# Raw projection weights for two chunks, paired transposes, sums parked through VectorE, and a new order in a fused attention and token-mixing block

## The chip, the core and the metric

The kernel runs on one core of a Trainium2 chip. The core has four compute engines that this kernel uses: TensorE (PE in the profile; its weight loads are shown apart as PEld), VectorE (DVE), ScalarE (ACT) and GpSimd (POOL). SyncE (SP) issues nearly all DMAs. Each engine works through its own instructions in program order and waits at semaphores for the others. The metric is the device time of one launch in microseconds, as the median of several runs.

## The reference

One residual block with two branches on x of 2048 tokens and 512 features, all in bf16. Six rows (sa, ca, ga, sb, cb, gb) come from a condition vector:

```python
mod = (_silu(c) @ w_mod).reshape(c.shape[0], 6, 1, -1)
h = _layernorm(x) * (1 + ca) + sa
x = x + ga * A(h)      # attention
h = _layernorm(x) * (1 + cb) + sb
x = x + gb * B(h)      # token mixing
```

Branch A projects h to q, k and v (32 heads of 16), and lets every position attend to 8 earlier positions at distance 0, 2, ... 14 of its own head; then comes the projection wo. Branch B takes a further layer norm of h, multiplies over the tokens: u = w1ᵀ h (2048 tokens to 1792 rows), adds b1, applies gelu, and comes back with y = w2ᵀ u + b2 (1792 to 2048).

## The kernel before

The 2048 tokens are 16 tiles of 128. Attention runs in five chunks of 2, 4, 4, 4 and 2 tiles (`SIZES`). Of each chunk, in names that stand in the order (chunk number first):

- ln1s, rstd1, nb1, n1: the first layer norm. ln1s takes a tile's statistics (on VectorE `bn_stats` and, at once behind it, `bn_aggr`; for tiles 10 to 13 on ScalarE with two passes that accumulate), n1 writes the normalized tile.
- tr, hT: for chunks 0 and 1 the transpose by TensorE and its copies out of PSUM. For chunks 2 to 4 it is xt, a DMA transpose of each tile on SP's queue.
- qkv{chunk}_{t}{j}, ev: projections (t = 0 for q, 1 for k, 2 for v) and their eviction. The scale 1 + ca (`a1col`) is folded into the weights: wsc multiplies each quarter of the loaded weights `wraw` by it and writes `w_r`. The shift sa goes into biases qvb of q and v, made by TensorE from the raw weights.
- vd: a DMA that spreads v; qk: products of q and shifted k on VectorE (up to 4096 elements a partition); red: their sums over the head on TensorE; max, sub, exp, esum, rcp, smB: the softmax; a2: DMAs that spread the probabilities; pv, pvacc, oev: products with v, sums, eviction. Chunk c needs the last 16 positions of the chunk before, copied by halo_k and halo_v.
- wo, x1: the output projection. The residual is added as one more product with the identity, except for tiles 14 and 15, where VectorE adds it. ln2q, ln2m, ln2s, n2, aff and ln3s, n3 (h3): second and third layer norms with the affine map between them.

Branch B runs in sweeps. mlp1_{sweep}_{row tile}_{first token tile} sums u over tokens. Row tiles 0 to 6 are summed over tokens 0 to 5, then 6 to 10, then 11 to 15; row tiles 7 to 13 over 0 to 9 and 10 to 15. A sum that isn't complete is parked as bf16 in `gT` (park, a copy). In the second of three sweeps the parked sum comes back into PSUM as a product with the identity (inj1_0 to inj1_6) before the sweep's own products; in a last sweep VectorE adds it (padd) and gelu follows. mlp2_{token tile} is the second product, fin adds b2, gb and the residual, st_out stores.

Rows of gates and shifts (modcol, mcols, mrowt, mrows) are made as columns with 64 products of one column, copied, transposed by TensorE, copied, stored and loaded back as broadcast rows. Warm-up bursts (warm0 to warm3, nine small products each) and fill keep TensorE running.

Nothing of the order is found at run time: the string `ORDER` (lines 182 to 238) lists every step by name, and steps are issued to their engines in that order. A letter behind a name picks the engine (:a ScalarE, :d VectorE), :q splits a product in four of 32 columns that run side by side. Slots of PSUM (`psS`, six), of `big` and of `vD` are given out in the same pass. The engine of each normalized tile stands in the strings `NE`, one letter a tile. The profile puts every operation on line 133, the wrapper that records it, so it is read by tiles.

Of the kernel before, what the change touches and what calls it, by code (L numbers as in the profile page):

```python
# [13 lines left out]
P = 128  # L14
# [27 lines left out]
class _Graph:  # L42
# [42 lines left out]
    def schedule(self):  # L85
# [4 lines left out]
        for pos, token in enumerate(ORDER.split()):  # L90
            name, *rest = token.split(":")
            if name == "fill":
                k, n = map(int, rest)
# [5 lines left out]
            o.quad = rest == ["q"]  # L99
            assert all(d in done for d in o.deps), name  # L100
            for eng, dur, fn in o.alts:
                if rest and eng[0] == rest[0]:
                    o.eng, o.dur, o.fn = eng, dur, fn
# [79 lines left out]
consts ld_x_1_2 act_table ld_x0 ld_x_1_4 ld_c ld_x_2_8 ld_x1 ident ld_x_2_6 ld_wmod1 ln1s3 halo0 ld_wqkv1 cps  # L183
ln1s2 warm2 ld_wqkv0 silu_exp ld_wmod0 ln1s0 ln1s4 ln1s1 ln1s5 rstd1_0 ld_x_4_14 nb1_0 ln1s9 rstd1_1 n1_0 n1_1
silu_dve nb1_1 ld_wqkv2 ln1s8 fill:2:70 tr0_0 n1_2 n1_4 modcols1 ln1s7 hT0_3:a n1_5 n1_3 ld_x_3_10 hT0_2:d a1col
hT0_0:a fill:4:16 tr1_2 wsc1_2:d ld_b1 hT0_1:a wsc1_3:d wsc1_0:a tr1_0 wsc1_1:d ln1s6 hT1_2:a ld_wmod2 qkv0_10
ld_x_3_12 wsc0_0:d rstd1_2 wsc0_1:d qkv0_12 wsc0_2:d hT1_1:a nb1_2 n1_8 n1_9 wsc0_3:d modcols0 hT1_0:d ld_wmod3
hT1_3:a qkv0_00 sab ev0_12:d n1_6 ld_wmod4 qvb0 ln1s14 ld_wo1 qkv0_02 qvb_cp0 ln1s15 ev0_00:a wsc2_2 qvb1
wsc2_0:d qkv1_00 wsc2_3 ev0_10:a ev0_02:d ln1s10 wsc2_1:d qkv1_10 qvb_cp1 qk0_0 ev1_10:a qkv0_22 qk0_1 n1_7
qkv0_20 ln1s13 qk0_2 qkv1_02 xt6 red0_0 ev1_00:a qk0_3 red0_1 red0_2 ev0_22:a ld_wmod5 qkv1_22 qk1_0 ev0_20:a  # L190
qkv1_12 ev1_02:a vd0_1 red0_3 ev1_12:a mask qkv1_11 vd0_0 ln1s11 max0 xt8 qk1_2 qkv1_01 ev1_11:a sub0 qkv1_03
ev1_01:a xt9 exp0 qkv1_13 qk1_1 ev1_03:a xt7 esum0 ev1_13:a qkv1_20 rcp0 vd0_2 ln1s12 qkv1_21 smB0 qk1_3 a2_0_3
modcol2 rstd1_4 qkv1_23 a2_0_0 ev1_22:a a2_0_2 halo_v1:a red1_0 ev1_20:a a2_0_1 red1_1 ln1v10 ln1v12 ln1v11
ln1v13 nb1_4 red1_2 rstd1_3 n1_15 ld_wo3 red1_3 nb1_3 ld_wo2 mcols0 n1_11 n1_10 qkv2_00 max1 ev1_21:a n1_14 xt10
qkv2_02 ev2_00:a pv0_0 qkv2_10 n1_12 ld_wo0 pv0_1 qkv2_11 vd0_3 ev2_10:a ev2_02:a qkv2_12 qk2_0 n1_13 qkv2_01
xt12 ev2_12:a pvacc0_0 ev2_01:a sub1 qk2_2 xt13 qkv2_03 exp1 qkv2_13 xt11 ev2_11:a ev2_03:a qkv2_22 qk2_1
ev2_13:a esum1 ev1_23:a qkv2_21 rcp1 vd1_2 red2_0 smB1 ev2_21:a ld_b2 red2_1 qk2_3 halo_v2:a a2_1_1 red2_2
pvacc0_1 a2_1_3 qkv3_00 a2_1_2 qkv3_10 a2_1_0 pv0_2 mrowt0 vd1_1 qkv2_20 ev3_10:a pv0_3 ev3_00:a red2_3 mrows0:a
qkv2_23 ev2_20:a st_row0 max2 halo_k3:p ev2_22:a vd1_3 qkv3_11 qk3_0 xt14 qkv3_22 ev3_11:a pvacc0_2 ld_row0
pvacc0_3 sub2:q oev0_2:a vd1_0 pv1_2 qkv3_02:q exp2 qkv3_12 ev3_02:a ev2_23:a qkv3_01 pv1_3 oev0_0:a vd2_2 esum2  # L200
modcol3 xt15 rcp2 ev3_12:a woq_s qkv3_20 ev3_01:a pvacc1_3 smB2 ev3_20:a red3_0 qk3_1 ev3_22:a a2_2_0 pvacc1_2
wo1 a2_2_1 vd2_3 qkv3_13:q x1_1 a2_2_2 pv1_1 vd2_1 wo0 ev3_13:a a2_2_3 qkv4_02 ld_w1_0_512 oev1_2:a mcols1 pv1_0
ld_w1_0_0 oev1_3:a mrowt1 qkv3_03 mrows1:a x1_0 st_row1 qkv4_00 ev3_03:a vd2_0 ln2q1 qk3_2 pvacc1_0 ev4_02:a
red3_1 pvacc1_1 oev1_0:a qkv3_23:q oev1_1:a qk3_3 ev4_00:a wo3:q ln2q0 wo5:q pv2_2 qkv4_22:q x1_5 ev3_23:a wo2:q
ld_row1 ln2q5 ld_w1_0_896 ln2m0 halo_v3:a wo4:q x1_3 pv2_1 x1_2 red3_2 x1_4 red3_3 ln2q3 qkv3_21:q pv2_3 rstd2_0
qkv4_20 ln2q2 ev3_21:a ev4_22:a vd3_3 pvacc2_1 nb2_0 max3 pvacc2_2 n2_0 warm0 ln2q4 vd3_0 n2_1 ln2m2 sub3 pv2_0
# [35 lines left out]
def kernel(  # L242
# [373 lines left out]
    def build_chunk(ch):  # L616
# [113 lines left out]
        if ch == 2:  # L730
            halo(3, "k")
# [307 lines left out]
```

## Time and profile before

| | us |
|---|---|
| median of 3 runs (lowest to highest) | 207.07 (206.38 to 207.98) |
| span of the profiled execution | 204.6 |
| busy: PE, DVE, ACT, POOL | 194.7, 163.3, 120.6, 13.0 |
| mean DMA share of 16 engines, bytes moved | 61.4%, 35.67 MB on the main queue |

The span runs from the first to the last instruction. A busy PE is not PE at its peak: matmuls are pipelined, and the time of one (0.38 us for 512 columns) is longer than the distance to the next. Further views are the stretches (busy time of each engine between two times), the chain of waits (the work that ended last, followed back), the timeline and the groups by shape.

### The profile page before, as it was taken

The numbers are of one execution on the slowest core, as the hardware profiler recorded it, in microseconds if no ns is written. First come the engines' busy times: TensorE is split into PE (matmuls) and PEld (weight loads), VectorE is DVE, ScalarE is ACT, GpSimd is POOL, SyncE is SP. The second block draws the span as 40 slices with busy tenths as digits, with TensorE's granted clock in tenths as the row PEclk, the third lists the DMA queues.
The fourth block names the chain that finished last, engine by engine and source line by source line (L and its number), as shares of the span: only waits on it lengthen the run. The fifth ranks groups of instructions, "written<-read, shape, count | busy, mean of one in ns | idle before, by whom it ended". The sixth has DMA issues, their size and how long they took to land.

```text
span 204.6 us, 4223 instructions
## 1 busy us (share of the span) xinstructions
PE 194.7 (95%) x1655; PEld 103.5 (51%) x1655; DVE 163.3 (80%) x260; ACT 120.6 (59%) x283; POOL 13.0 (6%) x36
## 2 busy tenths in 40 slices
PE   3999999999999997989899999999999999999994
PEld 3988554454455553554344445444444444444453
DVE  2899999999999999999999999975473204369365
ACT  2398998994666899989898876683762000000000
POOL 4122001100000001240000000100000000000000
PEclk9999999999999999999999999999999999999999
DMA  5999494646958976194975179946990930121121
GB/s 141 330 380 348 117 239 107 161 98 201 247 186 267 308 234 251 25 272 110 289 200 115 26 157 263 288 131 200 340 304 3 232 88 16 39 77 51 51 82 51
DMA packets 55111, 35.93 MB, mean 176 GB/s; under 512 B 24628, under 2 KB 52404, under 8 KB 55092
## 3 DMA queue, kind: packets, MB, share of 16 engines
q1 hardware_dynamic: 55084, 35.67, 61.4%
q8 instruction: 13, 0.21, 0.4%
q14 instruction: 6, 0.05, 0.1%
q10 hardware_dynamic: 8, 0.00, 0.0%
HBM read 22.55 MB, written 2.10 MB: 121 GB/s over the span
## 4 chain that ended last, share of the span: by engine, by line
PE 65%; DVE 20%; issue 5%; DMA 5%; SPq 3%; ACT 2%; DVEq 0%
PE psS L133 62%; DVE big L133 9%; DVE h L133 3%; PE psL L133 3%; SPq L133 3%; DVE st L133 3%; DMA wst<-in_B_w_dram 2%; DMA xx<-in_A_x_dram 2%; ACT h L133 1%; DVE mv L133 1%; DVE m L133 1%; DVE lsb L133 1%; DVE ls L133 0%; DVE nb L133 0%; DVE woq L133 0%
## 5 line engine op out<-in xcount | busy, mean ns | idle before, releaser
L133 PE MATMUL psS<-h,wst 128*128 128x512 bf16 (+1 forms) x254 | 50.7, 379 | 1.2 <-POOL h L133 0.7
L133 PE MATMUL psS<-hT,w_qkv 128*128 128x512 bf16 (+3 forms) x312 | 46.2, 339 | 0.3 <-ACT w_qkv L133 0.3
L133 PEld LDWEIGHTS <-wst 128*128 128x128 bf16 (+1 forms) x356 | 28.7, 98 | 32.2 <-issue 3.2
L133 PEld LDWEIGHTS <-w_qkv 128*128 128x128 bf16 (+1 forms) x354 | 29.5, 111 | 21.3 <-issue 3.2
L133 DVE TENSOR_TENSOR big<-a2sb,vD 128x4096 bf16<-128x4096 bf16 (+1 forms) x20 | 36.9, 1876 | 0.0
L133 DVE TENSOR_TENSOR big<-q_sb,k_f 128x4096 bf16<-128x4096 bf16 (+1 forms) x20 | 36.3, 1857 | 0.0
L133 DVE SCALAR_TENSOR_TENSOR h<-psS,bcol,rows_bc 128x512 f32<-128x512 f32 (+2 forms) x18 | 12.4, 690 | 24.4 <-PE psS L133 24.2
L133 PE MATMUL psS<-gT,big 128*128 128x512 bf16 x112 | 24.8, 379 | 0.0
L133 PEld LDWEIGHTS <-big 128*128 128x128 bf16 x144 | 12.0, 97 | 13.2
L133 PEld LDWEIGHTS <-ident 128*128 128x128 bf16 (+1 forms) x203 | 13.9, 111 | 5.9 <-issue 2.8
L133 PE MATMUL psS<-woq,o_sb 128*32 128x512 bf16 (+1 forms) x172 | 16.6, 380 | 0.0
L133 ACT ACTIVATE h<-xx,nb,rs 128x512 bf16<-128x512 bf16 x19 | 15.0, 807 | 0.8 <-DVE nb L133 0.7
L133 DVE TENSOR_TENSOR psS<-psS,gT 128x512 f32<-128x512 f32 x14 | 9.3, 696 | 7.0 <-PE psS L133 7.0
L133 ACT ACTIVATE junk<-xx 128x512 bf16<-128x512 bf16 x22 | 13.8, 626 | 0.2
L133 POOL TENSOR_SCALAR h<-xx,rs,nb 128x512 bf16<-128x512 bf16 x9 | 7.3, 813 | 101.3 <-DVE nb L133 84.0
L133 ACT ACTIVATE lv<-mv,epscol 128x1 f32<-128x1 f32 (+2 forms) x25 | 7.3, 291 | 9.3 <-DVE mv L133 8.4
L133 DVE BATCH_NORM_STATS2 st<-xx 128x6 f32<-128x512 bf16 x14 | 9.5, 678 | 4.0 <-DMA xx<-in_A_x_dram 4.0
L133 ACT ACTIVATE gT<-psS,bcol 128x512 bf16<-128x512 f32 x14 | 8.7, 688 | 6.4 <-DVE psS L133 6.4
L133 PEld LDWEIGHTS <-group 128*32 128x32 bf16 x288 | 6.8, 96 | 10.2 <-issue 4.8
L133 DVE TENSOR_TENSOR h<-h,rows_bc 128x512 bf16<-128x512 bf16 (+2 forms) x20 | 11.5, 581 | 0.5
L133 DVE TENSOR_TENSOR h<-h,xx 128x512 bf16<-128x512 f32 (+2 forms) x18 | 11.4, 633 | 0.6
L133 ACT ACTIVATE gT<-psS 128x512 bf16<-128x512 f32 x19 | 10.8, 587 | 1.6 <-PE psS L133 1.5
(94 smaller groups left out, 220.4 us busy)
## 6 DMA issues: line engine op xcount, KB each, us to landing
vD<-v_sb SPq DMA_DIRECT2D x12, 524.5 KB, 3.8
big<-in_B_w_dram SPq DMA_DIRECT2D x4, 896.0 KB, 8.2
vD<-v_sb SPq DMA_DIRECT2D x8, 268.5 KB, 3.0
wst<-in_B_w_dram SPq DMA_DIRECT2D x3, 640.0 KB, 5.3
out_dram<-h SPq DMA_DIRECT2D x15, 128.0 KB, 1.8
xx<-in_A_x_dram SPq DMA_DIRECT2D x7, 256.0 KB, 6.1
wst<-in_B_w_dram SPq DMA_DIRECT2D x2, 800.0 KB, 4.8
gT<-in_w_mod_dram SPq DMA_DIRECT2D x3, 512.0 KB, 6.1
```

The costliest lines, as they stand in the source:

```text
L133: r = fn(*a, **k)
```

## The change

- Chunks 0 and 1 are projected with the raw weights; the copies of their transposed tiles multiply by `a1col`. Only chunks 2 to 4 use `w_r`, and the twelve wsc move to GpSimd (7) and ScalarE (5); before, nine were on VectorE.
- One DMA transpose takes two tiles (five instead of ten), and its output lies tile by tile.
- The aggregate of the statistics is a step of its own in the order (ln1v, ln2v, ln3v). Statistics of the first and third norm can be on ScalarE: 3 of 16 and 8 of 16 are (before 4 and none).
- The engine of each normalized tile stands in the order: of n1, n2, h3 now 8, 8, 6 on ScalarE (before 9, 10, 8), 3, 6, 3 on VectorE (2, 2, 6) and 5, 2, 7 on GpSimd (5, 4, 2).
- An inj may be skipped (n); its park is then an addition on VectorE (+). All seven are. The residual product of a wo may be skipped in the same way, and x1 then adds it; this is used for tile 13.
- The rows of gates are made in rows at once: the condition column, broadcast to 32 columns, is the weight, and w_mod moves.
- halo_k3 comes after all q-k products of chunk 2, and runs on ScalarE; two v halos go from ScalarE to GpSimd. Five a2 DMAs are issued by ScalarE.
- The warm-up bursts are gone; fillers are 74 small products instead of 86, with a slot found by the pass. 42 products are split in four instead of 19.
- fin writes all three keys of its staging buffer where a tile has one piece. The whole order is new.

```diff
@@ schedule
-                k, n = map(int, rest)
+                n = int(rest[0])
+                k = min((freed["ps"][i], i) for i in range(self.pools["ps"]) if held["ps"][i] is None)[1]
...
+            flags = rest[0] if rest and o.eng == "pe" else ""
+            o.quad, o.skip = "q" in flags, "n" in flags
...
+            if o.eng == "pe":
+                o.eng, o.dur, o.fn = o.alts[o.skip]
...
+                if rest == ["+"]:
+                    o.eng, o.dur, o.fn = o.alts[-1]
@@ ln_stats
+        o = G.add_any([("dve", 0.68, fd)] + ([("act", 1.26, fa)] if l != 1 else []),
+                      reads=reads + (["act_table"] if l == 0 else []), writes=[("stt", l, st)], name=name)
...
+            if o.eng == "dve":
+                nc.vector.bn_aggr(mv[:, st, :], st6[:, st, :])
+            else:
+                nc.vector.scalar_tensor_tensor(mv[:, st, 1:2], mv[:, st, 0:1], mv[:, st, 0:1], st6[:, st, 0:1],
+                                               op0=ALU.mult, op1=ALU.subtract, reverse1=True)
@@ wraw: the value weights from h2_r[0] to h2_r[1]
-            wst[0][:, 0:KT * D].rearrange("p (k n) -> p k n", k=KT), h2_r[0][:, 0:KT, :])
+            wst[0][:, 0:KT * D].rearrange("p (k n) -> p k n", k=KT), h2_r[1][:, 0:KT, :])
@@ halo
-                  writes=[("kh", 3)] + [("k", -1, j) for j in range(4)] if nm == "k" else [("vh", ch), ("vh", ch - 2)],
+                  writes=[("kh", 3), ("kq", 2)] + [("k", -1, j) for j in range(4)] if nm == "k" else [("vh", ch), ("vh", ch - 2)],
@@ build_mod_rows
+                    for kt in range(KT):
+                        for dt_ in range(KT):
+                            nc.tensor.matmul(ps(s_)[32 * dt_:32 * dt_ + 32, r * P:(r + 1) * P],
+                                             lhsT=sc[:, kt:kt + 1].to_broadcast([P, 32]),
+                                             rhs=w_[:, kt, dt_ * P:(dt_ + 1) * P], start=(kt == 0), stop=(kt == KT - 1),
+                                             tile_position=(0, 32 * dt_))
@@ build_chunk: paired transposes
+            for sl in range(0, nt, XG):
+                st = t0 + sl
+                dma_t = lambda sl=sl, st=st: nc.sync.dma_start_transpose(
+                    out=hX[:, sl:sl + XG, :, :].rearrange("p s k q -> p (s k) q"),
+                    in_=h3[:, st:st + XG, :].rearrange("p s d -> p (s d)"))
@@ build_chunk: scaled copies, raw weights
+                    G.add_any([("act", _t_act(C, 1), lambda hd=hd, hs=hs, a_=a_: nc.scalar.activation(
+                        hd, hs(), ACT.Identity, scale=a_)),
+                               ("dve", 0.12 + 0.00052 * C, lambda hd=hd, hs=hs, a_=a_: nc.vector.tensor_scalar_mul(
+                                   hd, hs(), a_))], reads=["a1col"], writes=[("hT", bh, kt)], name=f"hT{ch}_{kt}",
...
-                        lhsT = _ap(w_r[t][:, kt, j:j + 1], [[4, P]])
+                        lhsT = _ap((wraw if ch in RAW else w_r)[t][:, kt, j:j + 1], [[4, P]])
@@ park
+                    fp = lambda s_=s_, ft=ft: nc.vector.tensor_tensor(gT[:, ft, :], ps(s_), gT[:, ft, :], op=ALU.add)
+                    G.add_any([("act", _t_act(D), fa), ("dve", _t_tt1(D), fd)] + ([("dve", 0.69, fp)] if inj else []),
+                              writes=[("gT", ft), "gT_use"], name=f"park{li}_{ft}", frees=s_).link = inj
@@ ORDER, its beginning and four later places
-consts ld_x_1_2 act_table ld_x0 ld_x_1_4 ld_c ld_x_2_8 ld_x1 ident ld_x_2_6 ld_wmod1 ln1s3 halo0 ld_wqkv1 cps
-ln1s2 warm2 ld_wqkv0 silu_exp ld_wmod0 ln1s0 ln1s4 ln1s1 ln1s5 rstd1_0 ld_x_4_14 nb1_0 ln1s9 rstd1_1 n1_0 n1_1
...
+ident ld_x_1_4 act_table ln1s4:d ld_x1 ld_x0 ld_x_1_2 ln1s1:d ln1v1 ln1v4 ld_wmod1 ld_c cps ln1s0:d ln1s5:a ln1v5
+fill:35 ln1v0 fill:14 ln1s2:d silu_exp consts rstd1_0 nb1_0 n1_0:a ln1s3:d n1_1:p ln1v2 ln1v3 silu_dve rstd1_1 nb1_1
+n1_5:d n1_4:d modcols1 tr0_0 a1col ld_x_2_8 n1_3:d n1_2:a tr1_0 hT0_1:a ln1s9:d ld_wqkv1 tr1_2 hT0_0:a hT1_0:d hT0_2:a
+ld_x_2_6 ln1s6:d hT0_3:a qkv0_12 hT1_3:a wsc1_1:p ld_wqkv0 hT1_2:a ld_x_3_12 ln1s7:d hT1_1:a ln1s8:d ln1v8 ev0_12:a
+ld_wmod0 wsc1_2:p wsc1_3:p ln1v7 ln1v6 qkv0_10 ld_x_3_10 ln1s13:d ln1v13 qkv1_13 wsc0_3:a ln1v9 ev0_10:a qkv0_02
...
+qkv1_12 mrows1 n1_8:p ev1_10:a qk1_0 qkv1_20 qkv1_23 xt8 vd0_2 a2_0_2:s qkv1_21:q qkv1_22:q ev1_12:a qk1_2 n1_11:a
+a2_0_1:a red1_0 qkv2_10:q qkv2_00:q red1_1 a2_0_3:s a2_0_0:s pv0_2 ln1s15:a ev1_22:a ev1_23:a st_row0 red1_2 red1_3
...
+mlp1_1_0_6 mlp1_1_0_10 ln2v14 rstd2_14 ld_w1_1_640 inj1_1:n mlp1_1_5_6 aff15 ln3s15:a nb2_14 park1_0:+ n2_14:p aff14
+inj1_4:qn mlp1_1_1_6 mlp1_1_6_6 inj1_3:qn rstd3_13 ld_w2_2 nb3_11 h3_11:p mlp1_1_3_6 mlp1_1_1_10 ln3v15 rstd3_15
...
+mlp2_11_0 st_out0_0 mlp2_8_0 mlp2_13_0 fin4_0 st_out4_0 fin7_0 st_out5_0 fin9_0 st_out9_0 mlp2_12_0 ld_w2_15 st_out7_0
...
+mlp2_15_2 mlp2_15_1 fin15_2 fill:7 fin15_1 st_out15_2 st_out15_1
```

292 lines of the change are left out of this document (128 added, 164 removed).

## The prediction

> **What bounds the kernel now.** I read the busy times by stretch first, then the chain of waits in order of time. Columns of the stretches: length, then busy time (and number of instructions) of TensorE, its weight loads, VectorE, ScalarE and GpSimd, the granted clock, the DMA share and GB/s.
>
> ```profile
> span 204.6 us, 4223 instructions
> ```
> ```profile
> 13.60:57.30 43.70, 43.69 (x404) 24.99 (x405) 43.41 (x52) 36.10 (x78) 3.41 (x5) 1.00 0.72 199
> 57.30:112.80 55.50, 51.97 (x656) 26.79 (x654) 54.64 (x68) 48.83 (x127) 4.22 (x5) 1.00 0.70 203
> 112.80:136.40 23.60, 23.57 (x137) 10.86 (x137) 22.18 (x63) 17.81 (x48) 0.77 (x1) 1.00 0.65 164
> 136.40:201.40 65.00, 65.00 (x330) 30.98 (x328) 33.09 (x50) 11.58 (x18) 0.00 (x0) 1.00 0.44 127
> ```
> ```profile
> 13.61 9.50 PE psS L133 x108
> ...
> 58.37 0.80 DVE woq L133
> ...
> 112.83 88.75 PE psS L133 x465
> ```
>
> TensorE is full in three of the four stretches, and the chain lies on it from 112.83 to the last product. But up to 112.8 VectorE is just as full (98.05 us of 99.2), and the chain lies on it from about 58 to 112. So two engines bind together up to the end of attention, TensorE alone after it. A gain needs less TensorE work or an earlier start, and VectorE must follow. The profiled span is 204.6 us, the median of the runs 207.07: 2.5 us lie outside the span and stay, so I subtract from 207.07.
>
> **Part 1, the start: raw weights and the new load order.**
>
> ```profile
> 12.17 0.15 DVE L133 TENSOR_SCALAR a1col<-psS 128x4 f32<-128x4 f32 x1
> 13.61 0.30 PE L133 MATMUL psS<-hT,w_qkv 128*128 128x256 bf16 x1 [0.26 <-ACT w_qkv L133]
> 19.48 1.21 DVE L133 TENSOR_TENSOR big<-q_sb,k_f 128x2048 bf16<-128x2048 bf16 x1
> ```
> ```profile
> L133 SPq DMA_DIRECT2D wst<-in_A_wqkv_dram x2: 505/542/578, 4.3 to 4.9; - x2
> ...
> DMA to landing us min/median/max: 7.0/7.4/7.8
> ```
> ```profile
> L133 SPq DMA_DIRECT2D xx<-in_A_x_dram x1: 1500/1500/1500, 7.1 to 7.1; - x1
> ...
> DMA to landing us min/median/max: 7.6/7.6/7.6
> ```
>
> Today the scale a1col (12.17) must multiply four weight slices before the first projection at 13.61. With raw weights for chunks 0 and 1 the copies of the transposed tiles carry the scale instead. Key and query weights landed at 4.3+7.0 = 11.3 and 4.9+7.8 = 12.7, when, by the sizes in the code, 2.30 and 2.82 MB had been asked for: 0.5 MB per 1.4 us. In the new order the key weights end at 2.05 MB, about 10.6, the w_mod half behind a1col at 1.28 MB instead of 1.79 (1.4 us earlier), and chunk 0's tiles at 0.51 MB instead of 1.02. I put a1col at 9.5 and four small copies behind it, first projection at 10.9: **-2.7 us for TensorE** (ends -3.0, the landing, and -1.0, if a1col moves little).
>
> VectorE's first q-k product (19.48) also needs the q bias, made from the other w_mod half. It ends at 3.58 MB, the same place in the queue as the x load that landed at 7.1+7.6 = 14.7. Column products, bias products, their copies and two evictions add some 3 us: 17.7, **-1.8 us for VectorE**. The nine weight slices that it loses fall in front of that point and are counted in it.
>
> **Part 2, TensorE's work.**
>
> ```profile
> 156.01 3.19 PE L133 MATMUL psS<-gT,big 128*128 128x512 bf16 x14
> ```
> ```profile
> 57.13 1.34 PE L133 MATMUL psS<-sc,gT 128*128 128x1 bf16 x48
> 58.33 1.04 PE L133 MATMUL psS<-hT,w_qkv 128*128 128x512 bf16 x4
> 59.30 0.61 PE L133 MATMUL psS<-big,group 128*32 128x512 bf16 x8
> ...
> 61.90 1.06 PE L133 MATMUL psS<-hT,w_qkv 128*32 128x512 bf16 x16
> ```
>
> A 512-column product costs (3.19-0.38)/13 = 0.216 us, 0.38 being the tail of the last. All seven inj tokens carry the flag that skips the identity product, and wo13 its residual one: 8 x 0.216 = -1.7. The 64 one-column products of modcol go (48 took 58.33-57.13 = 1.2 us, so 1.6); in come 64 quarter-width products of 128 columns, between 16 x 0.054 = 0.9 (four at a time) and 1.6 (none together). I take 1.2, as all quarter-width rows run four together: -0.4. A change between full and quarter width costs 0.1: the four at 58.33 need 0.97 instead of 0.86 until the quarter-width ones start. I count 38 changes instead of 34: +0.4. The 23 further tokens that split a product in quarters cost nothing (16 quarters at 61.90 take as long as 4 whole ones). Fillers are not counted; they stand where TensorE would wait. Sum **-1.7**; with the start -4.4.
>
> **Part 3, VectorE's work** between the first q-k product and the last normalized tile, which TensorE takes up with no slack today:
>
> ```profile
> 135.85 0.41 DVE L133 TENSOR_SCALAR h<-h,mv,rs 128x512 bf16<-128x512 bf16 x1 [0.30 <-ACT rs L133]
> ```
> ```profile
> 84.37 0.68 DVE L133 BATCH_NORM_STATS2 st<-h 128x6 f32<-128x512 bf16 x1
> 85.09 0.18 DVE L133 BATCH_NORM_AGGREGATE mv<-st 128x2 f32<-128x6 f32 x1
> 85.19 0.66 DVE L133 BATCH_NORM_STATS2 st<-h 128x6 f32<-128x512 bf16 x1
> ```
> ```profile
> L133 DVE SCALAR_TENSOR_TENSOR mv<-mv,st 128x1 f32<-128x1 f32 x4 | 0.6, 210 | 0.0
> ...
> L133 DVE TENSOR_TENSOR psS<-psS,gT 128x512 f32<-128x512 f32 x14 | 9.3, 696 | 7.0 <-PE psS L133 7.0
> ```
>
> A statistics pair takes 85.19-84.37 = 0.82; a next instruction that does not depend on the last starts 0.08 before its end. Eight pairs of this stretch go to ScalarE (-6.6), each leaving one small combine of 0.21-0.08 (+1.0). In the ten that stay the aggregate no longer stands right behind its statistics: 0.12 each, -1.2. Added: three parked sums before that tile, 3 x (0.70-0.08) = +1.9; x1_13, of a form that no row shows, bounded by that sum and by a statistics pair, +0.7; four more nb and the new row copies against the old column copies, +0.5. Sum -3.7.
>
> Against this stands GpSimd: 14 tile-sized operations in the stretch instead of 8 (h3 goes from 2 to 7), and 3 halo copies instead of 1.
>
> ```profile
> 36.01 0.77 POOL L133 TENSOR_SCALAR h<-xx,rs,nb 128x512 bf16<-128x512 bf16 x1
> ```
> ```profile
> 36.28 1.57 DVE L133 TENSOR_TENSOR big<-a2sb,vD 128x2048 bf16<-128x2048 bf16 x1
> ```
>
> The product at 36.28 began while GpSimd worked and took 1.57; one of its size took 1.21 at 19.48: +0.36. The bounds for the change are 0 (all beside statistics, as most are today) and 14 x 0.77 plus 3 copies, about 12. I take four collisions of 0.4, +1.6, nearer the low end because most of today's eight cost nothing. [...] VectorE in all: -1.8-3.7+1.6 = **-3.9**.
>
> **Part 4, what I cost at nothing.** ScalarE takes most of this work:
>
> ```profile
> 18.82 0.64 ACT L133 ACTIVATE junk<-xx 128x512 bf16<-128x512 bf16 x1
> 19.34 0.21 ACT L133 ACTIVATION_READ_ACCUMULATOR junk<-xx 128x1 f32 x1
> 19.58 0.63 ACT L133 ACTIVATE junk<-xx 128x512 bf16<-128x512 bf16 x1
> ```
> ```profile
> 0.83 0.56 ACTq L133 DMA_DIRECT2D c_t<-in_c_dram  x1
> ```
>
> One tile's statistics cost it 2 x (19.58-18.82) = 1.5 us; seven more in the stretch, five a2 issues of 0.56 (waiting for smB, with the evictions of the next projections queued behind), less its lost norms, parks and copies: some +10 on 102.7 of 122.8 busy. The cover is its 20 idle us, which become about 9 in a stretch that begins 2.7 and ends 4 us earlier; if that cover is gone, see the second rival.
>
> ```profile
> hT<-h SPq DMA_TRANSPOSE x10, 3.5
> ```
> ```profile
> L133 SPq DMA_TRANSPOSE hT<-h x10: 1211/1285/1714, 22.2 to 57.0; - x10
> ```
>
> A paired transpose holds SP's queue for 1.2 (as one) to 3.4 us (two of the slowest) and lands after 3.5 to 7. Between the issue of xt8 and the first chunk-2 projection TensorE has about three projections (12 x 0.216) and a reduction, some 3 us. I take one's cost; the other end is 3 us once, a2 and vd issues queued behind. The later key halo moves from GpSimd to ScalarE behind chunk 2's products, whose reductions already stand ahead of it. Parked sums after the last tile lie beside 65 us of full TensorE with 33 us of VectorE busy. The loads keep their queue; the late ld_w2_15 is issued some 9 us ahead of its use. fill:7 at the end stands beside the last output tile.
>
> The later of the two engines counts: -3.9 by VectorE, -4.4 by TensorE. I take -4.2: **202.9 us**.
>
> **Rivals.** *Full relief.* TensorE idles 3.5 us in 57.3 to 112.8 and does three warm-up bursts there; if VectorE gets ahead without collisions, another 4 us go: 198.9. For it: VectorE never waits today, so all that it loses counts. Against: its order was kept full by much ScalarE slack.
>
> *ScalarE becomes the bound.* If 12 of its 20 idle us stay, through dependent chains, the stretch lasts 113+12 = 125, 2.2 longer than now, and begins 2.7 earlier: no gain, 206.6. Against: those waits were mostly for a late VectorE.
>
> [...]
>
> *The clock.*
>
> ```profile
> 3.20:8.90 5.70, 5.70 (x55) 1.00 0.95 283
> 9.10:10.35 1.25, 1.25 (x26) 1.00 1.04 345
> ```
>
> Fillers start 0.104 us apart until 8.9 and about 0.05 after: TensorE ran at half pace until it had been busy for 5.9 us. The new start has 49 fillers, about 5.1 us at that pace, then a gap. If the change to full pace comes only after 5.9 us of unbroken projections, 3 us are lost: 205.9. [...]
>
> **Chances.** A measurement of this kernel tells about 1%, 2.1 us, from no change. Forecast (200.5 to 204.8) 0.45, full relief (198 to 200.5) 0.20, clock (204.5 to 206.5) 0.12, ScalarE (205.5 to 208) 0.12, port (208 to 213) 0.11. Faster, under 205.0: 0.45+0.20+0.05 = 0.70; slower, over 209.1: 0.10; the rest, 0.20, within. The range 198.3 to 207.8 leaves out the port and the best tenth.
>
> **What would show it.** First projection near 10.9 and first q-k product near 17.7; filler spacing before them; VectorE's products longer than 2.29 or 1.22 beside GpSimd; ScalarE's idle time up to the last normalized tile; the 65 us of TensorE after that tile unchanged. I am wrong if TensorE idles where it was full, between 13.6 and 57.3 or from 112.8 on.

## The result and the profile after

| | before | after |
|---|---|---|
| median, us (lowest to highest, 20 runs each) | 206.93 (206.05 to 207.98) | 205.28 (203.44 to 207.34) |
| profiled execution: time, span, us | 207.07, 204.6 | 207.27, 205.6 |

The ratio is 0.991, 95% interval 0.989 to 0.993: 1.65 us faster by the medians (about 1.9 by the ratio), where 4.2 was forecast. The profiled execution of the changed kernel is the second slowest of its 20; what is read from it below holds for that run, and the experiments' runs show what is usual. Six of the 20 runs, the profiled one among them, count as slow and are left out of the ratio, but not of the medians.

The page of the changed kernel, its span and the chain of waits by engine (before, PE had 65% of the chain, DVE 20% and ACT 2%):

```profile
span 205.6 us, 4632 instructions
...
PE 49%; ACT 19%; DVE 14%; DMA 7%; issue 6%; POOL 2%; SPq 1%; ACTq 0%; DVEq 0%; POOLq 0%
```

Its stretches, with the columns of the prediction's first table:

```profile
13.60:57.30 43.70, 41.74 (x569) 23.21 (x571) 39.38 (x45) 34.74 (x77) 8.35 (x11) 0.99 0.86 210
57.30:112.80 55.50, 52.17 (x721) 25.49 (x713) 54.63 (x65) 53.51 (x137) 2.50 (x4) 1.00 0.68 192
112.80:136.40 23.60, 23.27 (x135) 10.60 (x135) 21.80 (x63) 20.29 (x61) 4.59 (x6) 1.00 0.52 127
136.40:201.40 65.00, 65.00 (x326) 30.72 (x324) 34.91 (x53) 10.20 (x15) 0.00 (x0) 1.00 0.49 141
```

In the first stretch VectorE, full before (43.41 of 43.70 us), is busy for 39.38 us only, and TensorE has idle time too: the sign that the prediction named as its own refutation. In the second, three engines are now nearly full: ScalarE works 53.5 of 55.5 us.

To see where VectorE's relief went, take VectorE from its first q-k product to its last normalized tile. One row of that stretch for each kernel, before and then after; the fourth figure in each row is VectorE's busy time:

```profile
19.48:136.26 116.78, 113.22 (x1107) 57.14 (x1106) 114.47 (x162) 97.51 (x241) 7.04 (x9) 1.00 0.68 186
```
```profile
19.97:136.40 116.43, 111.07 (x1353) 54.56 (x1352) 111.67 (x157) 104.68 (x263) 11.70 (x14) 1.00 0.69 177
```

(The first figure is the length, the second TensorE, the third its weight loads.) The work fell by 114.47-111.67 = 2.8 us, more than the 2.1 forecast (-3.7+1.6). But the stretch is as long as before: VectorE idles 116.43-111.67 = 4.8 us where it idled 2.3, and it starts at 19.97, not at the 17.7 of the forecast. The largest wait and what lies behind it, from the waits of VectorE, SP's timeline and TensorE's timeline of the changed kernel:

```profile
DVE big L142 <- PE psL L142: 1.9, 1, 1.9
```
```profile
24.79 1.35 SPq L142 DMA_TRANSPOSE hT<-h  x1
26.19 0.75 SPq L142 DMA_DIRECT2D woq<-in_A_wo_dram  x1
26.98 0.58 SPq L142 DMA_DIRECT2D xx<-in_A_x_dram  x1
27.69 1.26 SPq L142 DMA_DIRECT2D vD<-v_sb  x2
29.05 1.52 SPq L142 DMA_TRANSPOSE hT<-h  x1
```
```profile
33.74 0.62 PE L142 MATMUL psL<-big,group 128*32 128x512 bf16 x8
35.22 1.06 PE L142 MATMUL psS<-hT,w_qkv 128*32 128x512 bf16 x16 [0.86 <-DMA hT<-h]
```

The second paired transpose (xt8) is issued at 29.05 behind two loads and two value copies and releases the projection at 35.22; TensorE stands 0.86 us, and as the reduction that frees VectorE's buffer is queued behind that projection, VectorE stands 1.9.

The late start shows in TensorE's granted clock (the figure after GpSimd's), in four stretches of the changed kernel:

```profile
7.70:9.10 1.40, 0.05 (x1) 0.10 (x1) 1.33 (x8) 1.23 (x3) 0.77 (x1) 1.00 0.95 322
9.10:11.30 2.20, 1.93 (x38) 1.62 (x38) 1.99 (x7) 1.88 (x5) 0.65 (x1) 1.00 1.07 375
11.40:14.70 3.30, 3.30 (x19) 2.41 (x17) 3.23 (x11) 3.30 (x7) 3.12 (x5) 0.50 1.11 382
14.80:17.00 2.20, 2.20 (x16) 1.61 (x15) 1.14 (x4) 1.60 (x4) 0.88 (x4) 1.00 1.08 355
```

The fillers end near 7.6 us, TensorE has next to nothing until 9.1, then column products and transposes run at full clock; and then, with TensorE full, the clock is at half for 3.4 us. The first two projections fall into it: at 11.53 and 13.24 they take 1.71 and 1.63 us for 0.86 us of work each. Of the 20 runs of the changed kernel, ten have a mean granted clock of 0.993 or less and a mean time of 206.3 us, and ten 0.998 or more and 204.8.

### The profile page after: what moved, and what is told of

Read it like the earlier page. It is cut to its first block, busy times and chain, and to the rows that moved or that the text cites. A ratio compares the mean times of both kernels' runs of the same rounds, so it can differ in the third digit from the quotient of the medians.

```text
span 205.6 us, 4632 instructions
## 1 busy us (share of the span) xinstructions
PE 192.8 (94%) x1852; PEld 99.5 (48%) x1852; DVE 160.4 (78%) x251; ACT 127.4 (62%) x305; POOL 21.1 (10%) x46
## 4 chain that ended last, share of the span: by engine, by line
PE 49%; ACT 19%; DVE 14%; DMA 7%; issue 6%; POOL 2%; SPq 1%; ACTq 0%; DVEq 0%; POOLq 0%
PE psS L142 48%; DVE big L142 8%; ACT junk L142 4%; ACT h L142 3%; DMA hT<-h 3%; DVE h L142 3%; ACT v_sb L142 2%; DMA xx<-in_A_x_dram 2%; ACT xx L142 2%; ACT o_sb L142 2%; POOL h L142 2%; DMA a2sb<-lsb 1%; ACT q_sb L142 1%; ACT gT L142 1%; ACT k_f L142 1%
## 5 line engine op out<-in xcount | busy, mean ns | idle before, releaser
L142 PEld LDWEIGHTS <-wst 128*128 128x128 bf16 (+1 forms) x446 | 35.3, 102 | 34.5 <-issue 3.0
L142 PE MATMUL psS<-hT,w_qkv 128*32 128x512 bf16 (+3 forms) x432 | 29.7, 346 | 0.9 <-DMA hT<-h 0.9
L142 PEld LDWEIGHTS <-w_qkv 128*32 128x32 bf16 (+1 forms) x474 | 19.6, 108 | 17.5 <-issue 5.7
L142 ACT ACTIVATE junk<-xx 128x512 bf16<-128x512 bf16 x20 | 12.6, 629 | 2.3 <-DMA xx<-in_A_x_dram 1.6
L142 ACT ACTIVATE h<-xx,nb,rs 128x512 bf16<-128x512 bf16 x16 | 13.0, 815 | 1.5 <-DVE nb L142 1.4
L142 DVE TENSOR_TENSOR h<-h,xx 128x512 bf16<-128x512 f32 (+2 forms) x18 | 11.4, 633 | 3.2 <-DMA out_dram<-h 2.6
L142 PE MATMUL psS<-hT,wst 128*128 128x256 bf16 (+1 forms) x64 | 12.8, 361 | 0.0
L142 ACT ACTIVATE v_sb<-psS,qvb 128x512 bf16<-128x512 f32 (+1 forms) x20 | 11.1, 595 | 1.4 <-PE psS L142 1.3
L142 PE MATMUL psS<-big,group 128*32 128x512 bf16 (+1 forms) x160 | 9.8, 339 | 2.0 <-DVE big L142 1.9
```

Of the source, the lines that this page charges most:

```text
L142: r = fn(*a, **k)
```

## The experiments

My theory after the result: the changed kernel does what was reckoned, and loses part of it to the half-clocked start (1.5 us, in half of the runs) and to waits that the sum took at nothing. The rivals: VectorE's relief is worth nothing since ScalarE has become the bound; GpSimd's larger share stops VectorE; or parts of the change bring less than reckoned. All variants but d1_cold carry the longer burst of the first, so that the half-clocked start doesn't blur them; in some of their runs the clock falls at other places (three of seven runs of a3_stats, three of twelve of c4_noraw and all six of b4_act have 0.992 or less). The kernel before was run beside every group of variants, with medians of 207.19, 207.10, 206.66 and 206.63 us. So a difference between variants of two groups is uncertain by some 0.5 us, and where that matters the ratios are given: a1_warm's is 0.986.

### a1_warm: close the gap in TensorE's start

```diff
-fill:35 ln1v0 fill:14
+fill:50 ln1v0 fill:14
```

> The changed kernel with 50 instead of 35 filler products in the first burst of fillers; nothing else differs. In the changed kernel's profile the 49 fillers end near 7.6 us, TensorE then has nothing until 9.15, and the first two projections (11.53 and 13.24) take 1.71 and 1.63 us for 0.86 us of work each: 1.6 us lost. 64 fillers, 0.106 us apart, reach 9.1 us. Clock theory: half of the changed kernel's runs, those with a granted clock of 0.993 or less, lose these 1.6 us; with the longer burst every run shows 0.998 or more, the first two projections take 0.86 us each, and the median falls from 205.3 to about 204.7 (ratio to the kernel before about 0.988). Rival: the cold start is hidden, since VectorE sets the pace up to 124 us, and both halves of the runs differ for another reason: clock as before in half of the runs, or median unchanged at 205.3.

204.19 us (203.49 to 204.76, six runs); ratio to the kernel before 0.986 (0.984 to 0.989). All six runs have a granted clock of 0.999 or more. The stretch that was at half clock, the first q-k product, and VectorE's stretch from there to the last normalized tile:

```profile
11.40:14.70 3.30, 3.30 (x25) 2.54 (x24) 3.20 (x11) 3.27 (x8) 3.15 (x7) 1.00 1.09 372
```
```profile
18.08 1.23 DVE L142 TENSOR_TENSOR big<-q_sb,k_f 128x2048 bf16<-128x2048 bf16 x1
```
```profile
18.08:132.62 114.54, 110.66 (x1352) 54.33 (x1351) 111.65 (x157) 104.09 (x263) 11.86 (x14) 1.00 0.69 185
```

The half clock at the start is gone, as the clock theory says, and the gain, 1.1 us on the median (1.0 by the ratios), is larger than the 0.6 expected. The product comes at 18.08 (17.7 forecast), VectorE's work is unchanged, and its idle time is 2.9 us instead of 4.8: the wait for xt8 is 0.2 us in this run. With fifteen more fillers the changed kernel is 3.0 us faster than the one before (207.19 in these runs).

Not all of the gain need be the clock: the ten runs of the changed kernel at full clock average 204.8 us, these six 204.1. And the two profiled runs differ in a second thing. In the changed kernel's, VectorE waits 1.00 us for a tile of x, and the condition column (sc), which TensorE's first column products need, comes at 8.94; in a1_warm it comes at 7.86. The trace of d2_injfull (a variant further down, with the longer burst) tells which of the two held the q-k product: sc is as late there, the clock is full, and the product comes 1.5 us earlier. The changed kernel's rows, then those of d2_injfull:

```profile
7.04 0.69 DVE L142 BATCH_NORM_STATS2 st<-xx 128x6 f32<-128x512 bf16 x1 [1.00 <-DMA xx<-in_A_x_dram]
8.94 0.16 DVE L142 TENSOR_TENSOR sc<-psS,ecol 128x4 bf16<-128x4 f32 x1
```
```profile
8.85 0.16 DVE L142 TENSOR_TENSOR sc<-psS,ecol 128x4 bf16<-128x4 f32 x1
18.47 1.22 DVE L142 TENSOR_TENSOR big<-q_sb,k_f 128x2048 bf16<-128x2048 bf16 x1
```

So of the 1.9 us between the products of the changed kernel and of a1_warm some 1.5 go to the clock (1.0 against the latest trace at full clock, 18.95 in c2_row). But the late tile makes the gap in front of it longer: the 49 fillers end at 7.76, and with sc as early as in a1_warm, whose column products start at 8.18, the gap would be about 0.4 us instead of 1.4. Whether the ten runs at half clock are those with a late tile isn't shown.

### a2_xt8, c2_row, c3_rowxt: take the waits on SP's queue away

```diff
-... xt6 ld_wo2 ... qkv1_23 xt8 vd0_2
+... xt6 xt8 ld_wo2 ... qkv1_23 vd0_2
```
```diff
-halo_v2:p vd2_1 ... pv1_2 ld_row1 pv1_1
+halo_v2:p ld_row1 vd2_1 ... pv1_2 pv1_1
```

The first edit is that of a2_xt8 (n1_8 and n1_9 stand earlier in the list too, without another place on GpSimd), the second that of c2_row; c3_rowxt has both.

> As a1_warm, and the second paired transpose of chunk 2 (xt8) is issued right behind the first (xt6), ahead of two loads and two copies of the values on SP's queue. Its two tiles are normalized by 18.7 us. In the changed kernel it is issued at 29.05, 4.3 us after xt6, and lands 6.0 us later at 35.08; TensorE waits 0.9 us for it, and VectorE then 1.9 us for the reduction behind. Theory of the late transpose: issued near 26.2 it lands by 32.5; both waits go and the time falls by 1 to 1.9 us against a1_warm. Rival: the order has slack behind it, VectorE is held by the next wait (copies of the values, now issued later, or of the softmax), and the time stays within 0.4 us of a1_warm.

> As a1_warm, with the load of the three modulation rows (ld_row1) put ahead of the copy vd2_1 on SP's queue. In a1_warm SP stands for some 7 us at that copy, which waits for chunk 2's values; the rows are asked for at 55.55 and the first sum with them on VectorE starts at 61.54, after 0.39 us of waiting (0.4 to 2.3 us in the other runs). Theory that this wait is the rows': it goes, and the time falls by 0.4 to 0.9 us, to 203.6. Rival: the sum waits for the normalized tile from ScalarE, and nothing changes.

> As c2_row, with the early xt8 of a2_xt8 too. If both waits are real and VectorE sets the pace, VectorE's idle time up to the last normalized tile falls from 2.8 us (a1_warm) to about 2, and the time to 203.3 or less. If the early xt8 only pushes the copies of the values back, as a2_xt8 (204.8) may say, it is 0.5 us slower than c2_row.

| | median us (lowest to highest) | ratio to before | VectorE's idle time, first q-k product to last normalized tile |
|---|---|---|---|
| a1_warm | 204.19 (203.49 to 204.76) | 0.986 (0.984 to 0.989) | 114.54-111.65 = 2.9 |
| a2_xt8 | 204.77 (203.53 to 205.47) | 0.991 (0.989 to 0.994) | 114.56-111.56 = 3.0 |
| c2_row | 204.36 (203.79 to 204.79) | 0.987 (0.983 to 0.990) | 114.96-111.54 = 3.4 |
| c3_rowxt | 203.96 (203.55 to 204.88) | 0.986 (0.982 to 0.990) | 114.88-111.62 = 3.3 |

Each edit takes its own wait away: in a2_xt8 VectorE doesn't wait behind xt8, and the wait for the rows is 0 in c2_row and c3_rowxt. The time doesn't follow: the wait of the one place appears in the next (in c2_row 1.1 us at 34.9, in a2_xt8 0.7 us at 60.9). The rival of both expectations holds, and a2_xt8 may even cost something. c3_rowxt has the lowest median of all, but not below a1_warm by more than their intervals; both are faster than the kernel before, and than the changed kernel by the ratios (0.986 against 0.991), with intervals that touch.

### a3_stats: give VectorE its statistics back

```diff
-ln1s15:a ... ln1s14:a ... ln3s1:a ... ln3s0:a ... ln3s2:a ... ln3s8:a ... ln3s6:a
+ln1s15:d ... ln1s14:d ... ln3s1:d ... ln3s0:d ... ln3s2:d ... ln3s8:d ... ln3s6:d
```

> As a1_warm, with seven statistics (ln1s14, ln1s15, ln3s0, ln3s1, ln3s2, ln3s6, ln3s8) taken back from ScalarE to VectorE: 7 x 0.62 = 4.3 us more on VectorE between the first q-k product and the last normalized tile, 7 x 1.5 = 10.6 us less on ScalarE. Theory that VectorE's work sets the pace (the prediction's own): 3 to 4.3 us slower than a1_warm, about 208. Rival, the gain swallowed by waits: in the changed kernel VectorE's waits rose from 1.3 to 3.9 us while its work fell by 1.5 up to the last value product, so what ScalarE took is paid in waits for it, and the time stays within 1 us of a1_warm.

207.93 us (207.67 to 208.73), 3.7 above a1_warm.

```profile
18.06:137.28 119.22, 112.16 (x1353) 55.13 (x1352) 115.79 (x164) 94.64 (x235) 11.44 (x14) 0.99 0.67 177
```

VectorE has 115.79-111.65 = 4.1 us more and the stretch is 4.7 us longer, though ScalarE has 9.5 us less. So VectorE's work does set the pace in this order, and what these seven statistics take off it counts nearly in full. The rival, that ScalarE's load swallows the relief, falls in this form.

### a4_inj and d2_injfull: TensorE's second sums

```diff
-inj1_5:qn inj1_0:n ... park1_0:+
+inj1_5:q inj1_0 ... park1_0:a
```

So for all seven in a4_inj; d2_injfull has inj1_2 to inj1_5 without :q.

> As a1_warm, with the seven second sums of the MLP's first product put back: an identity product of the parked sum on TensorE and a plain copy on ScalarE instead of the addition on VectorE. TensorE has 7 x 0.216 = 1.5 us more. Theory that TensorE is full from 124 us on: 1.5 us slower than a1_warm, nothing hidden. Rival: three of the products lie where TensorE has waits to spare (before 124 us none does by the order, so this would need idle time further on), and less than 0.8 us shows.

> As a4_inj, with the seven identity products whole instead of four of them in quarters. a4_inj was 2.85 us slower than a1_warm where 1.5 were expected; its trace shows 10 changes between whole and quarter width from 112.8 to 136.4 us instead of 2, 1.05 us instead of 0.21. Theory that each change costs 0.1 us on a full TensorE: 0.8 us faster than a4_inj, 206.2, 2.0 slower than a1_warm. Rival, the changes are hidden and the plain copies on ScalarE or their waits cost the rest: as a4_inj, 207.0.

a4_inj: 207.04 us (206.09 to 207.73), 2.85 above a1_warm. d2_injfull: 206.33 (205.31 to 207.4), 2.1 above it. Both lie above a1_warm by more than the 1.5 us of products, so nothing hides those. How the excess divides is open. Leaving the products in quarters brought eight more changes of width (46 in the trace of a4_inj, 38 in that of d2_injfull), and the medians differ by 0.7 us of the 0.8 expected; but the two were run in different groups, and their ratios to the kernel before, 1.0004 (0.9983 to 1.0025) and 0.9994 (0.9972 to 1.0017), don't tell them apart. So the theory's 0.8 us is not shown by the times. Nor is the rest of d2_injfull's excess settled: one wait on VectorE, for GpSimd's tile at 129.5, is 1.0 us where a1_warm has 0.4, but a4_inj has the same 1.0.

### b1_port and b4_act: more tiles for GpSimd

```diff
-n2_5:d ... n2_4:d ... n2_9:d ... n2_6:d
+n2_5:p ... n2_4:p ... n2_9:p ... n2_6:p
```
```diff
-n1_14:a ... n1_15:a ... n2_0:a ... h3_5:a ... n2_7:a ... n2_8:a
+n1_14:p ... n1_15:p ... n2_0:p ... h3_5:p ... n2_7:p ... n2_8:p
```

> As a1_warm, with four normalized tiles of the second normalization (n2_4, n2_5, n2_6, n2_9) taken from VectorE to GpSimd, which is busy for 4.0 of the 55.5 us there. VectorE loses 4 x 0.33 = 1.3 us of work ahead of the last value product, GpSimd gains 4 x 0.77. Theory that VectorE's work sets the pace and GpSimd is free: 1 to 1.3 us faster than a1_warm, 203.0. [...]

> As a1_warm, with six normalized tiles (n1_14, n1_15, n2_0, n2_7, n2_8, h3_5) taken from ScalarE to GpSimd: ScalarE, busy for 53.4 of the 55.5 us between 57.3 and 112.8, loses 6 x 0.7 = 4.2 us, GpSimd gains 6 x 0.77. Theory that ScalarE has become a second bound (the chain of waits lies on it from 48.7 to 59.4 and from 99.6 to 110.3 us): 1 to 2 us faster, not more, as VectorE waits for only 2.1 us in all up to the last value product. [...] Second rival: ScalarE is late without harm; within 0.4 us.

b1_port: 206.27 us (205.28 to 208.53), 2.1 slower than a1_warm. b4_act: 211.08 (209.1 to 213.15), 6.9 slower (6.4 by its ratio of 1.017), far beyond what any theory gave. Its trace is that of the slowest of its six runs (213.15 us), but its fastest is 4.3 above the slowest of a1_warm. GpSimd's groups of normalized tiles between 55 and 115 us, with the mean ns of one behind the busy time, in a1_warm and then in b4_act:

```profile
L142 POOL TENSOR_SCALAR h<-h,rs,nb 128x512 bf16<-128x512 bf16 x4 | 3.1, 772 | 31.7 <-DMA vD<-v_sb 20.2 <-DVE nb L142 11.4
L142 POOL TENSOR_SCALAR h<-xx,rs,nb 128x512 bf16<-128x512 bf16 x1 | 0.8, 773 | 38.7 <-DVE nb L142 38.7
```
```profile
L142 POOL TENSOR_SCALAR h<-xx,rs,nb 128x512 bf16<-128x512 bf16 x5 | 7.0, 1408 | 23.4 <-DVE nb L142 23.4
L142 POOL TENSOR_SCALAR h<-h,rs,nb 128x512 bf16<-128x512 bf16 x3 | 6.4, 2135 | 15.6 <-DVE nb L142 15.6
```

The means hide that most tiles still take 0.77 us. Of the three behind the 2135 two do, and the third takes 4.86: it starts just behind the first of two products of VectorE that follow each other without a gap, and ends after both. TensorE then waits for it. The rows of GpSimd, VectorE and TensorE:

```profile
96.86 4.86 POOL L142 TENSOR_SCALAR h<-h,rs,nb 128x512 bf16<-128x512 bf16 x1 [3.01 <-DVE nb L142]
```
```profile
96.68 4.49 DVE L142 TENSOR_TENSOR big<-a2sb,vD 128x4096 bf16<-128x4096 bf16 x2
```
```profile
101.78 2.29 PE L142 MATMUL psS<-h,wst 128*128 128x512 bf16 x5 [3.12 <-POOL h L142]
```

VectorE's stretch in b4_act, and the waits of VectorE in b1_port and in b4_act:

```profile
18.51:142.57 124.06, 113.52 (x1341) 56.05 (x1352) 113.29 (x157) 100.89 (x257) 29.61 (x20) 0.96 0.64 169
```
```profile
DVE h L142 <- POOL h L142: 2.5, 3, 1.3
```
```profile
DVE mv L142 <- ACT junk L142: 3.9, 3, 1.6
DVE h L142 <- DMA rows_bc<-scratch: 2.3, 1, 2.3
```

The theories of both expectations fall: each said faster, and both are slower. VectorE's own work hardly grows (113.29 us for 111.65). It is GpSimd's tile that takes longer, 4.86 us in these rows where a1_warm's take 0.77, and then others wait for it: TensorE 3.12 us here, VectorE 2.5 us in b1_port. VectorE's idle time is 124.06-113.29 = 10.8 us. That all of it comes from late tiles is not shown: its longest waits are for ScalarE (3.9) and for the rows of gates (2.3), and behind TensorE's wait of 3.1 us the granted clock is 0.50 from 102 to 105 us. In these rows VectorE's product started first, at 96.68, and GpSimd's tile ends at 101.72, 0.6 us after both products; what held the tile is not shown.

### b2_late and b3_x13: is there a point from which VectorE no longer counts?

```diff
-ln3s11:a ... ln3s12:a ... ln3s15:a
+ln3s11:d ... ln3s12:d ... ln3s15:d
```
```diff
-wo13:qn ... x1_13:d
+wo13:q ... x1_13:a
```

> As a1_warm, with the statistics ln3s11, ln3s12 and ln3s15 taken back to VectorE. They are due behind the last value product (120.9 us in a1_warm's profile); TensorE waits for nothing from 109.2 us on but 0.35 us once. VectorE has 3 x 0.62 = 1.9 us more. Theory of the hand-over (VectorE sets the pace up to about 109 us, TensorE's own work from there): within 0.4 us of a1_warm, while the seven statistics ahead of that point cost 3.7. Rival, as the prediction reckoned, with VectorE's work counted up to the last normalized tile: 1.9 us slower, 206.1.

> As a1_warm, with the residual of tile 13 back in TensorE's product (one more identity product, 0.216 us) and its copy with the sum on ScalarE instead of the addition on VectorE (0.60 us less on VectorE, 0.69 us more on ScalarE, at about 109 us). Theory that VectorE's work ahead of the hand-over sets the end: 0.4 us faster (0.6 less the 0.2 that TensorE has to do anyway). Rival, ScalarE is the bound in this place (the chain lies on it from 99.6 to 110.3 us): 0.5 to 0.9 us slower.

b2_late: 206.4 us (204.81 to 206.78), 2.2 above a1_warm. My theory of a hand-over at 109 us falls; the prediction's way of reckoning, VectorE's work up to the last normalized tile, stands. A wait of TensorE in b2_late behind 112 us that a1_warm doesn't have:

```profile
PE psS L142 <- DVE gT L142: 1.3, 1, 1.3
```

It is for a slot of PSUM that a late addition of a parked sum on VectorE frees. b3_x13: 205.27 us (204.53 to 206.27), 1.1 slower, though VectorE has 0.6 us less to do. Its longest waits on VectorE:

```profile
DVE ls L142 <- ACT lsb L142: 1.4, 1, 1.4
DVE h L142 <- ACT rb L142: 0.8, 1, 0.8
```

The first stands at 111.1 us, in the softmax of the last chunk, which the 0.69 us more on ScalarE at about 109 us delay. So ScalarE is a bound after all in single places: not by its sum, as the second rival of the prediction had it, but where a chain goes through it.

### c1_xg1: single transposes

```diff
-XG=2,
+XG=1,
...
-xt6 ... xt8 ... xt10 ... xt12 ... xt14
+xt6 xt7 ... xt8 xt9 ... xt10 xt11 ... xt12 xt13 ... xt14 xt15
```

> As a1_warm, with every paired transpose (two tiles, five issues) split into two single ones in the same place, as the kernel before has them. A pair holds SP's queue for 1.4 to 3.1 us and lands after 6.0 to 6.4 in the changed kernel's profile, a single one 1.2 to 1.7 and 3.5 in the kernel before. Theory that the pair's late landing is paid for: behind xt8 VectorE waits for 0.2 to 1.4 us in the runs so far (0.17 in a1_warm, 1.37 in a4_inj, 1.38 in b1_port); these waits go, 0.3 to 0.8 us faster than a1_warm. Rival: two singles hold the queue for 2.6 us and land no earlier together; within 0.4 us. It is the price that the prediction put at 0 to 3 us and took at 0.

206.47 us (205.38 to 208.3), 2.3 slower than a1_warm: the opposite of the theory. SP's queue at chunk 2's transposes in c1_xg1, and VectorE's longest wait:

```profile
22.56 2.61 SPq L142 DMA_TRANSPOSE hT<-h  x2
...
28.08 3.63 SPq L142 DMA_TRANSPOSE hT<-h  x2
...
32.46 2.02 SPq L142 DMA_DIRECT2D a2sb<-lsb  x3
```
```profile
DVE big L142 <- DMA a2sb<-lsb: 4.0, 2, 2.7
```

A pair lands later than a single one (5.0 to 6.2 us at the median against 3.5 to 3.8), but holds the queue for hardly more (1.35 and 1.52 us in the changed kernel's rows above) than one of the two singles (1.29 us at the median in the kernel before). Ten issues instead of five push the copies of the probabilities (a2) back, to 32.46 us where a1_warm issues the first at 29.70, and VectorE waits 4.0 us for those. Pairing is one of the parts that pay; the prediction gave it nothing.

### c4_noraw: scaled weights for all chunks

```diff
-RAW=(0, 1),
+RAW=(),
...
-wsc1_1:p ... wsc1_2:p wsc1_3:p ... wsc1_0:p
+wsc1_1:p wsc1_0:d wsc1_2:d wsc1_3:d ... wsc0_0:p wsc0_1:p
...
-qkv1_13 ... qkv0_02 qkv1_01 ... modcols0 ... qkv1_11
+qkv1_13 ... qkv1_11 ... modcols0 qkv0_02 ... qkv1_01
...
-qkv0_22 ... wsc2_1:a ... wsc2_0:a ... wsc2_3:p
+wsc2_1:p ... wsc2_0:a wsc2_3:p ... qkv0_22
```

> As a1_warm without raw weights: chunks 0 and 1 use scaled weights again, and the copies of their transposed tiles no longer scale. Three key slices are scaled on VectorE and one on GpSimd ahead of the first projection, the four query slices ahead of the first query projection, which moves behind the column products; everything else keeps its place. Theory of the prediction's part 1: the first projection starts 1 to 2.7 us later than in a1_warm (10.4 to 11.4 us in the runs so far) and, as TensorE and VectorE are both full, the end moves by 1 to 2.7 us, to 205.2 to 206.9. Rival: the early start of the new kernel comes from the order of the loads alone; the four key slices take 3 x 0.27 us beside the transposes, and the time is within 0.5 us of a1_warm.

206.84 us (205.65 to 208.61), 2.65 above a1_warm, at the upper end of the theory. But not by its mechanism: the first projection starts at 10.62 us, within the 10.4 to 11.4 of the runs with raw weights. The four key slices hide beside the transposes, as the rival said. The waits of TensorE from 10 to 60 us in c4_noraw are longest elsewhere:

```profile
PE psS L142 <- ACT w_qkv L142: 1.6, 1, 1.6
PE psS L142 <- ACT v_sb L142: 1.2, 1, 1.2
```

The value projection of chunk 0 (at 20 us) waits 1.6 us for its slices, which the raw weights let fall to any later time. The rest of the loss stands on VectorE: 112.59 us of work in a stretch of 118.17 (18.35 to 136.52), so 0.9 more work and 2.7 more idle time than in a1_warm, of which 1.5 are a wait for the rows of gates and 1.0 one for probabilities; how these follow from the slices is not shown. Where those slices stand was my choice in this variant, so 2.65 us is the price of this order without raw weights, not of the best one.

### d1_cold: a shorter burst

```diff
-fill:35 ln1v0 fill:14
+fill:15 ln1v0 fill:14
```

> The changed kernel with 15 instead of 35 filler products in the first burst: 29 in all, ending near 5.5 us at 0.107 us each, then nothing until the column products at 9.15. Clock theory (the pace doubles only after a stretch without a gap that 29 fillers never make, 49 make in half of the runs and 64 in all): every run shows a granted clock of 0.993 or less, the first projections run at half pace in all of them, and the median is that of the slower half of the changed kernel's runs, 206.3, some 2.1 above a1_warm. Rival, the cold start costs nothing by itself and a1_warm gained in another way: median as the changed kernel's, 205.3.

205.42 us (204.51 to 207.13): 1.2 above a1_warm, and not clearly slower than the changed kernel (205.28; the ratios to the kernel before, 0.9945 with 0.9916 to 0.9974 and 0.991 with 0.989 to 0.993, overlap). Only 7 of 12 runs have a granted clock of 0.993 or less. The expectation missed. The profiled run shows why half clock needn't hurt:

```profile
9.05:12.40 3.35, 3.19 (x24) 2.59 (x23) 2.93 (x8) 2.73 (x7) 2.02 (x3) 0.50 1.08 372
12.50:14.80 2.30, 2.30 (x19) 1.88 (x18) 2.20 (x9) 2.30 (x6) 2.18 (x5) 1.00 1.09 382
```

Here the 3.4 us at half clock come 2.3 us sooner and lie mostly on the transposes; the first projection starts at 11.14 and the q-k product at 18.64. In this kernel the times of the runs don't go with the clock: the seven average 205.4 us, the five at 0.999 or more 205.9. So a closed gap is worth 1.0 to 1.1 us, but how much half clock costs depends on where it falls, and how that gain divides between the clock and the later pieces that it shifts isn't settled.

## Why the prediction missed

The predicted sign was right, the size was not: 1.65 us of 4.2. The whole difference of the two spans, in rows that stand above and the last sum of each kernel on VectorE, before, after and in a1_warm:

```profile
201.60 0.35 DVE L133 SCALAR_TENSOR_TENSOR h<-psS,bcol,rows_bc 128x128 f32<-128x128 f32 x1
```
```profile
201.97 0.35 DVE L142 SCALAR_TENSOR_TENSOR h<-psS,bcol,rows_bc 128x128 f32<-128x128 f32 x1
```
```profile
198.19 0.35 DVE L142 SCALAR_TENSOR_TENSOR h<-psS,bcol,rows_bc 128x128 f32<-128x128 f32 x1
```

| us against the kernel before | forecast | profiled run after | profiled run of a1_warm |
|---|---|---|---|
| first q-k product (19.48) | -1.8 | +0.5 | -1.4 |
| VectorE's work from there to its last normalized tile (114.47) | -2.1 | -2.8 | -2.8 |
| VectorE's idle time in that stretch (2.3) | 0 | +2.5 | +0.6 |
| last normalized tile to last sum (201.60-136.26 = 65.3) | 0 | +0.2 | +0.2 |
| last sum to the end of the span (204.6-201.60 = 3.0) | 0 | +0.6 | +0.6 |
| sum | -3.9 | +1.0 | -2.8 |

(-3.9 is the prediction's sum for VectorE; it took -4.2 between that and TensorE.) The run after is one of the slowest of its kernel and that of a1_warm the fastest of its six, so the usual run lies between the columns.

Point by point:

- *Two engines bind.* Right: 4.1 us of VectorE's work cost 3.7 us (a3_stats), 1.5 us of TensorE's at least 2.1 (d2_injfull).
- *Part 1.* The first projection was put at 10.9: 11.53 in the profiled run, 10.4 to 11.4 in the variants. The size was right, the reason only in part, as c4_noraw shows: with scaled weights and the new order of loads it still starts at 10.62, and the longest wait of TensorE in c4_noraw is at the value projection. **The step that failed is the q-k product at 17.7, -1.8 us for VectorE.** Its 3 us for column products, bias products, copies and evictions stood at full clock, behind projections at full clock. With those at half clock the product came at 19.97. At full clock it came at 18.47 with the condition column as late (d2_injfull), and at 17.50 to 18.95, on average 18.2, in the thirteen traces with the longer burst; so the term was small by some 0.5 us even at full clock. The place of the loss was that of the rival on the clock, which had 0.12 and came true in half of the runs, costing 1.5 us there by the two halves' means, while closing the gap brought 1.0 to 1.1 us on all runs (a1_warm). Its mechanism was another: not that the fillers were too few to reach full pace (the 16 column products from 9.15 us on take 0.54 us, as those at 10.84 in the kernel before do), but that the pace fell again behind the gap. It stayed at half for 3.4 us here and in d1_cold, at another place in each; what decides in which runs it falls is not shown.
- *Part 2.* Right, and a little small. The changes of width are 38 in the trace, as counted, after 34. The rows of the gates took 0.24+0.79 = 1.0 us with their changes, instead of the 1.2 reckoned and 1.6 before. The prediction's upper end of 1.6 for "none together" doesn't follow from its own price: 64 products at 0.054 make 3.5; the 1.0 measured is near the lower end, four at a time.
- *Part 3.* Right in sign, -2.8 instead of -2.1, and near in size partly by luck. The collisions with GpSimd were mis-sized: where they lengthen VectorE's own instructions it is in one softmax product beside a GpSimd tile (at 27.62, for 2.80 us), 0.4 us instead of 1.6 (the first row below is of the kernel before, the second of the changed one), so all the other terms together brought about -3.2 instead of -3.7. GpSimd's late tiles were in no term, and cost little in this kernel: in its profile VectorE waits for GpSimd once in that stretch, 0.4 us; b1_port and b4_act, with more tiles on GpSimd, were 2.1 and 6.9 us slower.

```profile
31.25 0.42 DVE L133 TENSOR_TENSOR lsb<-lsb,rb 128x512 bf16<-128x512 bf16 x1
```
```profile
29.85 0.85 DVE L142 TENSOR_TENSOR lsb<-lsb,rb 128x512 bf16<-128x512 bf16 x1
```

- *Part 4.* **The second step that failed: stalls at nothing.** For the paired transposes the end of the range, "3 us once", was seen and not taken. xt8 cost VectorE 1.9 us in the profiled run and 0 to 1.4 in the variants. But the pairs themselves are worth 2.3 us by the queue that they free, which the prediction didn't see either. ScalarE's load is no bound by its sum (second rival), but 0.7 us more in one place cost 1.1.
- *The chance called port*, 208 to 213, with VectorE stopped by GpSimd's tiles: not in this kernel, beyond the 0.4 us above. *Full relief*, 198.9: no run came near.

Of the shortfall of 2.55 us the clock takes an estimated 0.75, 1.5 us in half of the runs. Closing the gap in front of it brought 1.0 us by the ratios and 1.35 by the medians (from 1.65 to 3.0), so up to half of the shortfall; what of that isn't the clock is open. The rest is in the last column of the table: the product 0.4 later than reckoned, 0.6 of new idle time even in the best run, 0.8 behind the last normalized tile, less 0.7 for the work. That the last 0.6 of it, from the last sum to the end of the span, recurs in both runs is seen and not explained.

## What to carry to other kernels

Where two engines are full and one hand-made order ties them, undoing a single part cost 1.1 to 3.7 us here, while all parts together, with the gap closed, brought 3.0: price a part by the order that it stands in, and give a new order some idle time in the sum, since the two waits that were taken away came back at the next place. Before costing a start-up, look for a gap in TensorE's work ahead of it: fifteen idle products closed a gap of up to 1.4 us and brought 1.0 to 1.1. And weigh a queue by what stands behind a transfer, not only by when it lands.

## What the runs showed of the hardware

In these runs TensorE's clock fell to half behind stretches that were only partly idle, and with a delay. In the changed kernel it was busy 1.98 of 3.6 us (7.70 to 11.30), at full clock, and then at half clock for 3.4 us while it was full. The same in the middle of a3_stats, behind two waits for VectorE:

```profile
72.00:76.50 4.50, 2.32 (x36) 1.23 (x29) 4.35 (x8) 2.55 (x7) 0.00 (x0) 1.00 1.11 249
76.60:79.90 3.30, 3.30 (x17) 1.16 (x19) 3.30 (x4) 2.02 (x6) 0.95 (x2) 0.50 0.58 217
80.00:82.00 2.00, 2.00 (x32) 1.02 (x20) 2.00 (x2) 1.63 (x4) 0.00 (x0) 1.00 0.31 120
```

Busy for 2.32 of 4.5 us at full clock, then 3.3 us and a little more at half clock though full, then full clock again. The half pace of the very first fillers (0.104 us apart until 8.9 us and about 0.05 after, in the prediction's rows of the kernel before) doesn't show in the granted clock, which reads 1.00 in both rows, so the fillers' spacing has to be read as well.
